# Two layers of dilated attention and GeGLU: chunks of 256 rows throughout, first roots on POOL, low parts on DVE, bulk loads on ACT's queue, a new order

## The chip, the cores and the metric

The kernel runs on one core of a Trainium2 chip. The metric is the device time of one execution in microseconds; the number compared is the median of several runs. A profiled execution has a time of its own and a span, from its first to its last instruction.

## The reference

Four sublayers are applied to x (2048 rows of 512 numbers): attention, feed-forward, and both again with the same weights. Every one has a layer norm in front and a residual around it.

```python
x = x + A(layernorm(x), wqkv, wo)              # wqkv 512 x 1536, wo 512 x 512
x = x + B(layernorm(x), w_gate, w_up, w_down)  # 512 x 1792, 512 x 1792, 1792 x 512
x = x + A(layernorm(x), wqkv, wo)
x = x + B(layernorm(x), w_gate, w_up, w_down)

# A: 32 heads of 16; row s sees the 8 rows s, s-2, ..., s-14 (those below 0 are masked)
qkv = h @ wqkv
logits[s, w] = (q[s] . k[s - 2*w]) / 4
o[s] = sum_w softmax(logits[s])[w] * v[s - 2*w]
A = o @ wo
# B:
B = (gelu(h @ w_gate) * (h @ w_up)) @ w_down
```

## The kernel before

**Chunks.** Because the window steps by 2, even and odd rows never meet. A chunk is `128*J` rows of one parity; `TILES` (line 36) gives the sizes J of both layers: `[1, 1, 2, 2, 2]` in the first, `[2, 2, 2, 2]` in the second, each for both parities. The first layer has 10 chunks, four of them of 128 rows, the second 8 of 256 rows.

**Numbers in two parts.** TensorE multiplies float16. Each operand is a high part (rounded) and a low part (the rest); a product is three passes: high by high, high by low, low by high. Weights are scaled by powers of two first, found from their largest magnitudes: `prep_q`, `prep_f`, `prep_o` and `prep_d` (lines 485 to 598) load a weight (`load`, line 461, on SP's queue), take magnitudes (`absmax` on DVE, L469; `abssum` on ACT, L479), get exponents (`exponents`, L373 to L393, with a transpose on PE, L380), and `split` each block of 128 rows. `split` has three ways: "v", ACT makes the high part from the raw block (L425) and DVE the low part (L430); "p", ACT scales the raw block in place (L436), ACT makes the high part (L446), POOL the low part (L450); the third, POOL scales. Only w_q uses "v". w_q's raw blocks lie in the space of w_d, so w_d is loaded after w_q is split.

**A chunk's way.** `attention_inputs` (line 767): load rows (`load_xa`, three buffers, L654), `norm` (line 662): statistics on DVE (L677, L681), then the reciprocal root by an integer first guess and three Newton steps, 13 small DVE instructions (L704 to L723); ACT normalises (L752); `split_transpose` (line 728) makes high (ACT, L735) and low part (POOL, L739) and turns them with a transposing DMA on SP (L743) into `ax`; PE projects, per half of the heads and row tile in 12 matmuls of 512 columns and 12 of 256 (L763 with w_q), ACT evicts to `stg` (L802), SP stores to DRAM (L813). `attention` (line 820): per group of 8 heads SP loads q and windows of k and v (L840); DVE multiplies (L858), sums (L865), softmax (L876 to L911, ACT's exponential L897), multiplies with v (L917), adds up (L928, L933); the result is split and transposed into `ot`. `feed_forward` (line 945): output projection (L763 with w_o), residual on DVE (L970), `norm` again, `bx`; then seven steps of two column blocks: gate and up (L763 with w_g, w_u), GELU on ACT (L1018), product on DVE (L1026), high part on ACT (L1035), low part on POOL (L1040), down projection (L1051); last the residual (L1064) and a store (L1072) to `xs`, from which the second layer reads, or to the output.

`passes` (L763) issues all matmuls but the down projection, so in the profile these groups are told apart by their tiles.

**The order.** Nothing is issued in the order of this text. Each operation is a node in `Graph` with its engine, a duration, the keys that it reads and writes, buffers to take (`Lease`) and a priority. `plan` (line 138) places node after node on a model of the five engines: of those that can start, the earliest; among those within `WAIT` = 0.3 us of it, one whose priority number is over `SOON` = 20 smaller goes first. It models one DMA stream, and holds a load on SP back until the stream's backlog is under `QUEUE` = 4 us. The instructions are then written out in that order (lines 1096 to 1099), and every engine executes its own in order; an instruction whose data is late holds all behind it. Priorities are in us: the feed-forward pass of a chunk is due at T, which starts at 100 and grows by 38 per 128 rows; attention at T - 90 and on, first inputs of the first chunks 8 apart, later ones at T - 170 (lines 1078 to 1094).

Of the kernel before, what the change touches and what calls it, by code (L numbers as in the profile page):

```python
# [35 lines left out]
TILES = ([1, 1, 2, 2, 2], [2, 2, 2, 2])  # L36
# [46 lines left out]
QUEUE = 4.0  # L83
# [168 lines left out]
def dilated_attention_geglu(ctx: ExitStack, tc: tile.TileContext, x, wqkv, wo, wg, wu, wd, out):  # L252
# [208 lines left out]
    def load(dst, src, kb, w, prio, r=()):  # L461
        return g.add(
            "SP", T_ISSUE + 0.0006 * kb, lambda: nc.sync.dma_start(dst, src), r=r, w=w, kb=kb, prio=prio
        )
# [95 lines left out]
    def prep_o(prio, how):  # L560
        for k in range(KT):
            load(w_o.raw(k), wo[k * P : (k + 1) * P], 256, [(P_o_lease, k)], prio)
        for k in range(KT):
            h = k // (KT // 2)
            abssum(
                am_o[:, h, k % (KT // 2) : k % (KT // 2) + 1], w_o, k, (P_o_lease, k), ("am_o", k), prio + 5
            )
        e = exponents("o", am_o, [("am_o", k) for k in range(KT)], prio + 5)
        su, cst["s_wo"] = meet(
            "o", e, e_v, -127 - 19, [("o", "e"), ("s_log", 0), ("s_log", 1)], prio + 5  # L570
        )
        for k in range(KT):
            h = k // (KT // 2)
            split(w_o, k, su[:, h : h + 1], ("su_o", 0), how[k % len(how)], prio + 6, (P_o_lease, k))

    def load_d(prio):
        for i in range(NF):
# [3 lines left out]
                r=[("q", b) for b in range(2 * KT)],  # L581
# [80 lines left out]
    def norm(xs_of, prio):  # L662
# [12 lines left out]
        for j in range(J):  # L675
# [13 lines left out]
        ts, stt = nc.vector.tensor_scalar, nc.vector.scalar_tensor_tensor
# [2 lines left out]
        def op(fn, r, w):
            def emit():
                st, mv, cs = view()
                fn(mv, cs)
# [6 lines left out]
        g.add(  # L702
            "DVE port", 0.15,
            lambda: ts(view()[2][V], view()[1][:, :, 1], EPS, 2.0 ** (-2 * LX), op0=ALU.add, op1=ALU.mult),  # L704
            r=[(lease, *k) for k in mvs], w=[(lease, V)], prio=prio,
        )
        op(
            lambda mv, c: ts(
                c[Y].bitcast(I32), c[V].bitcast(I32), -0.5, float(0x5F3759DF), op0=ALU.mult, op1=ALU.add
            ),  # L710
            [V], [Y],
        )
        op(lambda mv, c: ts(c[HF], c[V], -0.5, None, op0=ALU.mult), [V], [HF])
        for k in range(3):
            dst = Y if k < 2 else SC
            op(lambda mv, c: nc.vector.tensor_mul(c[WK], c[Y], c[Y]), [Y], [WK])
            op(lambda mv, c: nc.vector.tensor_mul(c[WK], c[WK], c[HF]), [HF], [WK])
# [410 lines left out]
```

## Time and profile before

| | us |
|---|---|
| median of 3 runs | 1308.7 |
| lowest, highest | 1306.49, 1309.39 |
| the profiled execution, its own time | 1306.3 |
| its span | 1304.5 |
| busy in it: PE | 1230.2 (94%) |
| DVE | 1025.8 (79%) |
| ACT | 542.2 (42%) |
| POOL | 388.9 (30%) |
| mean granted TensorE clock | 0.98 |

PE is the row of matmuls and PEld that of weight loads beside them. A busy PE need not be PE at its peak, since matmuls are pipelined and their ends are modelled; how fast they follow one another is seen in the chain and the timeline. Idle time of an engine that is not the bound costs nothing by itself. SPq is SP's queue of DMA issues. Lines such as L763 are lines of the kernel before.

### The profile page before, as it was taken

Reading aid. Unit: us, or ns where it says so; the run is one execution under the profiler, and the core shown is the slowest. Engines: PE = TensorE matmul, PEld = TensorE weight load, DVE = VectorE, ACT = ScalarE, POOL = GpSimd, SP = SyncE. Lnnn points to the kernel's source line nnn. Section 1 sums busy time; section 2 is a strip of 40 time slices with the busy share of each in tenths; the row PEclk is TensorE's granted clock in tenths of the full one; section 3 lists DMA queues with packets and bytes.
Section 4 is the critical chain, followed back from the end, with each engine's and each line's share of the span. In section 5 each row is a group of like instructions: output and inputs, shape, how many; then the busy total and the mean of one; then the engine's idle time right before and its main releaser. Section 6 shows DMA issues by size and latency. Waiting matters only on the chain.

```text
span 1304.5 us, 23267 instructions
## 1 busy us (share of the span) xinstructions
PE 1230.2 (94%) x9322; PEld 861.2 (66%) x9322; DVE 1025.8 (79%) x1762; ACT 542.2 (42%) x832; POOL 388.9 (30%) x307
## 2 busy tenths in 40 slices
PE   2796889998699999999999999999999999999998
PEld 1453558775575777767757777765677677667775
DVE  7878878999998898898998888934889898886211
ACT  5587465443334352435434343332444342322211
POOL 1374263332333242423313322211232224222111
PEclk9897999999799999999999999999999999999999
DMA  9977825774538443335439343317834433231000
GB/s 328 357 212 203 243 82 167 230 181 150 132 112 192 138 122 122 121 122 149 137 129 245 87 121 111 129 41 177 228 81 130 123 122 103 90 120 41 17 17 17
DMA packets 205581, 183.58 MB, mean 141 GB/s; under 512 B 108928, under 2 KB 170368, under 8 KB 205472
## 3 DMA queue, kind: packets, MB, share of 16 engines
q1 hardware_dynamic: 205408, 181.97, 48.0%
q8 instruction: 73, 1.20, 0.4%
q14 instruction: 36, 0.29, 0.1%
q10 hardware_dynamic: 64, 0.11, 0.0%
HBM read 123.21 MB, written 33.67 MB: 120 GB/s over the span
## 4 chain that ended last, share of the span: by engine, by line
PE 74%; DMA 0%; DVE 0%; DVEq 0%; issue 0%; SPq 0%
PE pg L763 54%; PE pd L1051 19%; DMA bx<-hl 0%; DVE x L1064 0%; DVEq L1123 0%; SPq L743 0%
## 5 line engine op out<-in xcount | busy, mean ns | idle before, releaser
L763 PE MATMUL pg<-bx,w_g 128*128 128x256 f16 (+1 forms) x3024 | 338.0, 262 | 20.6 <-DMA bx<-hl 16.1
L763 PE MATMUL pg<-bx,w_u 128*128 128x256 f16 (+1 forms) x3024 | 337.2, 262 | 0.0
L763 PEld LDWEIGHTS <-w_g 128*128 128x128 f16 x3024 | 272.3, 98 | 69.3 <-issue 17.1
L1051 PE MATMUL pd<-w_d,gh 128*128 128x512 f16 x1344 | 310.4, 380 | 5.6 <-POOL w_d L450 5.5
L763 PEld LDWEIGHTS <-w_u 128*128 128x128 f16 x3024 | 271.7, 98 | 26.9
L1040 POOL TENSOR_TENSOR gh<-g,gh 128x512 f16<-128x512 f32 (+1 forms) x126 | 168.3, 1336 | 398.4 <-ACT gh L1035 375.9
L763 PE MATMUL pg<-w_q,ax 128*128 128x512 f16 (+1 forms) x1536 | 262.6, 333 | 23.9 <-DMA ax<-hl 20.4
L763 PEld LDWEIGHTS <-ax 128*128 128x128 f16 x1536 | 152.3, 99 | 134.7 <-DMA ax<-hl 22.5
L1051 PEld LDWEIGHTS <-gh 128*128 128x128 f16 x1344 | 130.9, 98 | 144.6 <-issue 8.0
L1026 DVE SCALAR_TENSOR_TENSOR g<-pg,small,g 128x512 f32<-128x512 f32 (+2 forms) x144 | 89.0, 629 | 151.9 <-ACT g L1018 148.6
L1018 ACT ACTIVATE g<-pg,small 128x512 f32<-128x512 f32 (+2 forms) x144 | 83.5, 593 | 228.7 <-PE pg L763 227.8
L917 DVE TENSOR_TENSOR prod<-v,lg 128x1024 f32<-128x1024 f32 x128 | 165.3, 1315 | 0.9
L739 POOL TENSOR_TENSOR hl<-xn,hl 128x512 f16<-128x512 f32 x64 | 84.1, 1322 | 268.6 <-ACT hl L735 241.9
L858 DVE TENSOR_TENSOR prod<-k,q 128x2048 f32<-128x2048 f32 (+1 forms) x72 | 152.1, 2112 | 3.1 <-DMA k<-qkvd 2.5
L928 DVE TENSOR_TENSOR prod<-prod 128x512 f32<-128x512 f32 (+2 forms) x144 | 151.3, 1051 | 1.6
L865 DVE TENSOR_REDUCE lg<-prod 128x128 f32<-128x2048 f32 (+1 forms) x72 | 146.8, 2039 | 0.7
L739 POOL TENSOR_TENSOR hl<-o,hl 128x256 f16<-128x256 f32 (+1 forms) x72 | 81.5, 1133 | 209.4 <-ACT hl L735 157.8
L1035 ACT CAST gh<-g 128x512 f16<-128x512 f32 (+1 forms) x126 | 71.8, 570 | 77.5 <-DVE g L1026 75.6
L802 ACT ACTIVATE stg<-pg 128x768 f32<-128x768 f32 x64 | 51.6, 811 | 125.8 <-PE pg L763 120.4
L1018 ACT ACT_TABLE_LOAD x53 | 68.0, 1283 | 80.8 <-PE pg L763 80.3
L763 PE MATMUL pg<-w_o,ot 128*128 128x512 f16 x384 | 85.8, 379 | 0.0
L897 ACT ACT_TABLE_LOAD x52 | 66.7, 1283 | 0.9
(71 smaller groups left out, 717.5 us busy)
## 6 DMA issues: line engine op xcount, KB each, us to landing
k<-qkvd SPq DMA_DIRECT2D x56, 576.0 KB, 4.1
v<-qkvd SPq DMA_DIRECT2D x56, 576.0 KB, 3.4
qkvd<-stg SPq DMA_DIRECT2D x64, 384.0 KB, 3.6
k<-qkvd SPq DMA_DIRECT2D x16, 512.0 KB, 4.3
v<-qkvd SPq DMA_DIRECT2D x16, 512.0 KB, 3.9
q<-qkvd SPq DMA_DIRECT2D x56, 128.0 KB, 2.0
xa<-in_A_x_dram SPq DMA_DIRECT2D x16, 256.0 KB, 5.2
xa<-xs SPq DMA_DIRECT2D x16, 256.0 KB, 6.1
```

The lines of the kernel that those rows point to most:

```text
L739: "POOL", t_pool(n), lambda: nc.gpsimd.tensor_sub(lo(), src(), hi()),
L763: nc.tensor.matmul(pt, a, b, start=i == 0, stop=i == n - 1)
L858: nc.vector.tensor_mul(pr, win, q.tile()[:, 0:J].unsqueeze(2).to_broadcast([P, J, W, P]))
L865: lambda lgv=lgv: nc.vector.tensor_reduce(lgv(), pr.rearrange("p j w (h d) -> p j w h d", d=DH), axis=AX.X, op=ALU.add),
L897: lambda lgv=lgv, scale=scale: nc.scalar.activation(lgv(), lgv(), AF.Exp, scale=scale),
L917: lambda j=j, v=v, lg=lg: nc.vector.tensor_mul(prod[:, j].rearrange("p w (h d) -> p w h d", d=DH), v.tile()[:, j : j + W].rearrange("p w ( ...
L928: lambda a=a, b=b: nc.vector.tensor_add(pr[:, :, 0:a], pr[:, :, 0:a], pr[:, :, a:b]),
L1018: lambda sel=sel, h=h, pg=pg, gt=gt: nc.scalar.activation(gt.tile()[:, sel, 0:N], pg.tile()[:, sel, 0:N], AF.Gelu_apprx_tanh, scale=cst["s ...
L1026: lambda sel=sel, h=h, pg=pg, gt=gt: nc.vector.scalar_tensor_tensor(gt.tile()[:, sel, 0:N], pg.tile()[:, sel, JM * P : JM * P + N], cst["c ...
L1035: lambda gt=gt, gh=gh: nc.scalar.copy(gh.tile()[:, 0, :, 0:N], gt.tile()[:, :, 0:N]),
L1040: lambda gt=gt, gh=gh: nc.gpsimd.tensor_sub(gh.tile()[:, 1, :, 0:N], gt.tile()[:, :, 0:N], gh.tile()[:, 0, :, 0:N]),
L1051: nc.tensor.matmul(pd.tile()[:, j], gh.tile()[:, a, i, cs], wd_of(f, b), start=f == 0 and n == 0, stop=f == NF - 1 and n == 2,)
```

## The change

It has five parts.

1. `TILES` gives all chunks of both layers 256 rows: 8 chunks a layer.
2. `norm` gets an engine. For the attention inputs, all but those of the very first chunk, the small instructions after the statistics are eight on POOL, with a power function in place of the guess and the Newton steps. The norm before the feed-forward pass stays on DVE.
3. Gate and up are split by way "v" in place of "p".
4. `load` can issue on ACT's queue: the loads of w_g, w_u, w_o and w_d (34 DMAs) go there. Loads of x and w_q stay on SP. The planner models two streams that share the rate.
5. Priorities come from a table `AT`; weight loads and weight preparation have separate ones, and the first magnitudes are taken first.

```diff
-TILES = ([1, 1, 2, 2, 2], [2, 2, 2, 2])
+TILES = ([2, 2, 2, 2], [2, 2, 2, 2])
...
+AT = dict(
+    lq0=0.0, lq1=1.4, lf0=6.0, lo=42.0, lf1=52.1, ld=60.0, pq0=-787.8, pq1=2.6, pf0=21.6, po=53.4, pf1=59.2,
+    pd=130.5, x0=-1000.0, first=0.0, tile=9.1, ahead=8.5, lead=218.0, norm=300.0, proj=18.6, half=14.0,
+    row=8.0, att=90.0, hg1=6.5, hg2=12.0, kv=33.0, xl=30.6, gu=5.6, start=51.1, step=39.1,
+)
...
-QUEUE = 4.0
+QUEUE = {"SP": 4.0, "ACT": 8.0}
...
-        dma_free, port_free, table = 0.0, 0.0, None
+        dma, port_free, table = {"SP": 0.0, "ACT": 0.0}, 0.0, None
...
-                    if e == "SP" and n.size is not None and not n.urgent:
-                        t = max(t, dma_free - QUEUE)
+                    if n.size is not None and not n.urgent:
+                        t = max(t, dma[e] - QUEUE[e])
...
-                begin = max(t + occ, dma_free)
-                dma_free = begin + n.size / DMA_RATE
-                n.done = dma_free + DMA_FIXED
+                other = "ACT" if e == "SP" else "SP"
+                begin = max(t + occ, dma[e])
+                both = min(max(0.0, dma[other] - begin), 2 * n.size / DMA_RATE)
+                dma[e] = begin + n.size / DMA_RATE + both / 2
+                dma[other] += both / 2
+                n.done = dma[e] + DMA_FIXED
...
+    root = sb.tile([P, JM], F32, name="root")
+    nc.gpsimd.memset(root, -0.5)
...
-    def load(dst, src, kb, w, prio, r=()):
-        return g.add(
-            "SP", T_ISSUE + 0.0006 * kb, lambda: nc.sync.dma_start(dst, src), r=r, w=w, kb=kb, prio=prio
-        )
+    def load(dst, src, kb, w, prio, r=(), on="SP"):
+        eng = nc.sync if on == "SP" else nc.scalar
+        return g.add(on, T_ISSUE, lambda: eng.dma_start(dst, src), r=r, w=w, kb=kb, prio=prio)
...
+        else:
+
+            op(lambda m, v, c: ts(c[V], v, EPS, None, op0=ALU.add), mvs, [V])
+            op(lambda m, v, c: tt(c[Y], c[V], root[:, 0:J], op=ALU.pow), [V], [Y], 0.4 + 0.17 * J)
+            op(lambda m, v, c: tt(c[WK], c[Y], c[Y], op=ALU.mult), [Y], [WK])
+            op(lambda m, v, c: tt(c[WK], c[WK], c[V], op=ALU.mult), [V], [WK])
+            op(
+                lambda m, v, c: ts(
+                    c[WK], c[WK], -(2.0 ** (LX - 1)), 1.5 * 2.0**LX, op0=ALU.mult, op1=ALU.add
+                ),
+                [], [WK],
+            )
+            op(lambda m, v, c: tt(c[SC], c[WK], c[Y], op=ALU.mult), [WK, Y], [SC])
+            op(lambda m, v, c: tt(c[HF], m, c[SC], op=ALU.mult), [SC], [HF])
+            op(lambda m, v, c: ts(c[BI], c[HF], -1.0, None, op0=ALU.mult), [HF], [BI])
...
-        nl, sb_of = norm(xt, prio - 300)
+        nl, sb_of = norm(xt, prio - AT["norm"], "DVE" if l + c == 0 else "POOL")
...
-            prio = T - 90 + (10 if J == 2 else 5) * hg
+            prio = T - AT["att"] + (AT["hg2"] if J == 2 else AT["hg1"]) * hg
...
-    prep_f(0, 25.0, "p")
-    prep_o(40.0, "p")
+    prep_f(0, AT["pf0"], "v")
+    prep_o(AT["po"], "p", AT["lo"])
...
-    prep_f(1, 60.0, "p")
+    prep_f(1, AT["pf1"], "v")
...
-    t, first = 100.0, 0.0
+    t, tiles = AT["start"], 0
     for l in range(2):
         for c, (par, t0, J) in enumerate(CHUNKS[l]):
-            attention_inputs(l, c, -1000.0 if l + c == 0 else first if l == 0 and first < 72 else t - 170)
+            if l + c == 0:
+                when = AT["x0"]
+            elif l == 0 and tiles < AT["ahead"]:
+                when = AT["first"] + AT["tile"] * tiles
+            else:
+                when = t - AT["lead"]
+            attention_inputs(l, c, when)
             ot, mark = attention(l, c, t)
             feed_forward(l, c, t, ot, mark)
-            t += 38.0 * J
-            first += 8.0 * J
+            t += AT["step"] * J
+            tiles += J
```

More of the change, by code (lines that the diff above doesn't have):

```diff
@@ L514, in load_f @@
                 i = h * KT + k
-                load(w.raw(i), src[h, k], 448, [(f"r{key}", i)], prio + 0.1 * k)
+                load(w.raw(i), src[h, k], 448, [(f"r{key}", i)], prio + 0.1 * k, on="ACT")
     def prep_f(h, prio, how):
@@ L558, in meet, with prep_o @@
         return su, s
-    def prep_o(prio, how):
+    def prep_o(prio, how, early):
         for k in range(KT):
-            load(w_o.raw(k), wo[k * P : (k + 1) * P], 256, [(P_o_lease, k)], prio)
+            load(w_o.raw(k), wo[k * P : (k + 1) * P], 256, [(P_o_lease, k)], early, on="ACT")
         for k in range(KT):
@@ L565, in prep_o @@
             abssum(
-                am_o[:, h, k % (KT // 2) : k % (KT // 2) + 1], w_o, k, (P_o_lease, k), ("am_o", k), prio + 5
+                am_o[:, h, k % (KT // 2) : k % (KT // 2) + 1], w_o, k, (P_o_lease, k), ("am_o", k), prio
             )
-        e = exponents("o", am_o, [("am_o", k) for k in range(KT)], prio + 5)
+        e = exponents("o", am_o, [("am_o", k) for k in range(KT)], prio)
         su, cst["s_wo"] = meet(
-            "o", e, e_v, -127 - 19, [("o", "e"), ("s_log", 0), ("s_log", 1)], prio + 5
+            "o", e, e_v, -127 - 19, [("o", "e"), ("s_log", 0), ("s_log", 1)], prio
         )
@@ L573, in prep_o @@
             h = k // (KT // 2)
-            split(w_o, k, su[:, h : h + 1], ("su_o", 0), how[k % len(how)], prio + 6, (P_o_lease, k))
+            split(w_o, k, su[:, h : h + 1], ("su_o", 0), how[k % len(how)], prio + 1, (P_o_lease, k))
     def load_d(prio):
@@ L580, in load_d @@
                 w_d.raw(i), wd[i * P : (i + 1) * P], 256, [("rd", i)], prio + 0.1 * i,
-                r=[("q", b) for b in range(2 * KT)],
+                r=[("q", b) for b in range(2 * KT)], on="ACT",
             )
@@ L660, in load_xa, with norm @@
         return got
-    def norm(xs_of, prio):
+    def norm(xs_of, prio, on="DVE"):
         J = len(xs_of)
@@ L687, in norm, with op @@
             g.add("DVE", 0.17, aggr, r=[(lease, "st", j)], w=[(lease, "mv", j)], prio=prio)
[L689 removed]
         V, HF, WK, Y, SC, BI = range(6)
[L692 removed]
+        eng = nc.vector if on == "DVE" else nc.gpsimd
+        ts, tt = eng.tensor_scalar, eng.tensor_tensor
+        stt = nc.vector.scalar_tensor_tensor
+        def op(fn, r, w, occ=None):
             def emit():
[L694 to L695 removed]
+                _, mv, cs = view()
+                fn(mv[:, :, 0], mv[:, :, 1], cs)
@@ L696, in op @@
             return g.add(
-                "DVE port", 0.15, emit, r=[(lease, k) for k in r], w=[(lease, k) for k in w],
-                prio=prio,
+                "DVE port" if on == "DVE" else "POOL", occ or (0.15 if on == "DVE" else 0.19), emit,
+                r=[(lease, *k) if isinstance(k, tuple) else (lease, k) for k in r],
+                w=[(lease, k) for k in w], prio=prio,
             )
         mvs = [("mv", j) for j in range(J)]
[L702 to L717, printed above, removed]
-            op(
-                lambda mv, c, dst=dst: stt(c[dst], c[WK], 1.5, c[Y], op0=ALU.add, op1=ALU.mult),
-                [WK, Y], [dst],
-            )
@@ L797, in attention_inputs @@
                     r=[(ax, j), *(("q", h * KT + k) for k in range(KT))], w=[(pg, 0)],
-                    get=[pg], prio=prio + 25 + 16 * h + 8 * j,
+                    get=[pg], prio=prio + AT["proj"] + AT["half"] * h + AT["row"] * j,
                 )
@@ L947, in feed_forward @@
         N = J * P
-        xt, xl = load_x(l, c, T - 45, order=[mark])
+        xt, xl = load_x(l, c, T - AT["xl"], order=[mark])
         pw = Lease(P_pg)
```

48 lines of the change are left out of this document (33 added, 15 removed).

## The prediction

> **What bounds the kernel now.** I read the page's slices first, then a table of stages, then PE's waits and the chain that ended last. The slices give the busy tenths of PE in fortieths of the span (32.6 us each):
>
> ```profile
> PE   2796889998699999999999999999999999999998
> ```
>
> All gaps but the last lie in the first eleven slices. The table of stages gives length, busy time (and instructions) of PE, weight loads, DVE, ACT and POOL, then granted clock, DMA share and GB/s:
>
> ```profile
> 0.00:60.00 60.00, 30.09 (x133) 14.82 (x134) 47.71 (x151) 31.19 (x48) 13.32 (x18) 0.91 1.02 338
> 60.00:140.00 80.00, 67.23 (x398) 39.21 (x397) 64.69 (x134) 60.42 (x102) 45.21 (x30) 0.91 0.79 231
> 140.00:200.00 60.00, 49.97 (x522) 36.90 (x521) 47.72 (x116) 37.01 (x66) 29.01 (x28) 0.91 0.46 140
> 200.00:340.00 140.00, 123.89 (x1327) 90.09 (x1325) 127.44 (x246) 63.04 (x110) 44.22 (x42) 0.94 0.62 176
> 340.00:640.00 300.00, 300.00 (x2206) 215.90 (x2205) 265.95 (x416) 123.04 (x177) 96.74 (x68) 1.00 0.48 137
> 640.00:940.00 300.00, 300.00 (x2094) 204.66 (x2092) 235.17 (x361) 113.31 (x162) 69.21 (x56) 1.00 0.49 137
> ...
> 1240.00:1304.50 64.50, 59.06 (x436) 42.37 (x433) 8.20 (x12) 9.31 (x15) 8.09 (x8) 0.99 0.05 17
> ```
>
> From 340 us on PE never stops, at full clock; before, it is idle 68.8 us (340 less 30.09, 67.23, 49.97 and 123.89), and 5.4 us at the end: 74.2 in all. Its waits by cause (total, times, longest):
>
> ```profile
> PE pg L763 <- DMA ax<-hl: 20.4, 4, 11.6
> PE pg L380 <- DVE small L373: 18.8, 3, 12.2
> PE pg L763 <- DMA bx<-hl: 16.1, 1, 16.1
> PE pd L1051 <- POOL w_d L450: 5.5, 4, 1.9
> ```
>
> So PE's own work is the bound, plus what it waits for in the first quarter. What that work is at full speed: in the chain (start, length, matmuls) a run of 256-wide matmuls costs 5.24/48 = 0.1092 us each,
>
> ```profile
> 357.89 5.24 PE pg L763 x48
> ```
>
> and one of 512-wide 5.18/24 = 0.2158:
>
> ```profile
> 394.39 5.18 PE pd L1051 x24
> ```
>
> The counts by form (the busy times beside them are of pipelined matmuls and not used):
>
> ```profile
> L1051 PE MATMUL pd<-w_d,gh 128*128 128x512 f16 x1344 | 310.4, 380 | 5.6 <-POOL w_d L450 5.5
> L763 PE MATMUL pg<-bx,w_g 128*128 128x256 f16 x2352 | 290.0, 273 | 16.1 <-DMA bx<-hl 16.1
> L763 PE MATMUL pg<-bx,w_u 128*128 128x256 f16 x2352 | 289.1, 273 | 0.0
> L763 PE MATMUL pg<-w_q,ax 128*128 128x512 f16 x768 | 184.3, 390 | 23.9 <-DMA ax<-hl 20.4 <-ACT w_q L425 1.6 <-DVE w_q L430 1.2
> L763 PE MATMUL pg<-w_q,ax 128*128 128x256 f16 x768 | 96.0, 276 | 0.0
> L763 PE MATMUL pg<-w_o,ot 128*128 128x512 f16 x384 | 85.8, 379 | 0.0
> L763 PE MATMUL pg<-bx,w_u 128*128 128x128 f16 x672 | 48.1, 223 | 0.0
> ```
>
> With every chunk at 256 rows, gate and up (two equal halves) become 2 x (2352 + 672/2) = 5376 matmuls of 256. The new PE work is (5376 + 768) x 0.1092 = 670.9 us plus (1344 + 768 + 384) x 0.2158 = 538.6, together 1209.5; per chunk 75.6, of which projection 15.6, output projection 5.2, feed-forward 54.8. The present work is the same but for halves of 128 in place of 256, which I price at nothing. Then the span holds 1209.5 of work, 74.2 idle and, as the remainder, 20.8 of slow clock (0.91 to 0.94 in those stages) and of starting up after pauses. Only idle and slow time can be gained.
>
> **Part by part. Chunks of 256 rows** take instructions from DVE:
>
> ```profile
> L858 DVE TENSOR_TENSOR prod<-k,q 128x2048 f32<-128x2048 f32 x56 | 130.8, 2336 | 3.1 <-DMA k<-qkvd 2.5
> ...
> L858 DVE TENSOR_TENSOR prod<-k,q 128x1024 f32<-128x1024 f32 x16 | 21.2, 1327 | 0.0
> ```
>
> Two half-size products cost 2 x 1.327 - 2.336 = 0.32 us more than a whole one. Over some 12 instructions and 8 pairs of head groups that is at most 31 us; I take 22, as reductions and short ones will save less; all of it lies before 340 us. The price: the first chunk's attention is twice as long, and no feed-forward pass can start after 128 rows.
>
> **Roots on POOL.** 15 of the 16 first normalisations lose 13 small DVE instructions, which are not only time but are spread out. One such chain, its first and last instruction:
>
> ```profile
> 113.52 0.16 DVE L704 TENSOR_SCALAR nw<-nw 128x2 f32<-128x2 f32 x1
> ...
> 121.47 0.15 DVE L723 SCALAR_TENSOR_TENSOR nw<-nw 128x2 f32<-128x2 f32 x1
> ```
>
> Here 13 x 0.16 = 2.1 us of work took 8.1, queued between attention instructions. POOL's eight, with a power function, are not in the trace. The nearest, a 128-wide and two 512-wide subtractions:
>
> ```profile
> 125.83 0.43 POOL L739 TENSOR_TENSOR hl<-o,hl 128x128 f16<-128x128 f32 x1 [10.68 <-DMA v<-qkvd]
> 126.49 2.27 POOL L739 TENSOR_TENSOR hl<-xn,hl 128x512 f16<-128x512 f32 x2 [0.24 <-POOL hl L739]
> ```
>
> Bounds for eight: near nothing, and 8 x 1.13 = 9 us. I take 8 x 0.43 = 3.4, since two columns are nearest to the small one: between DVE's 2.1 and its 8.1. After 340 us PE's other work hides it; without that cover the upper bound adds 6 us for each of the first four chunks, 24 us.
>
> **Low parts of gate and up on DVE**, priced by those of w_q:
>
> ```profile
> L430 DVE SCALAR_TENSOR_TENSOR w_q<-w_d,small,w_q 128x768 f16<-128x768 f32 x8 | 9.5, 1238 | 0.4 <-ACT w_q L425 0.4
> ```
>
> 16 x 1.238 x 896/768 = 23 us more DVE work before about 170 us. ACT loses a scaling pass,
>
> ```profile
> L436 ACT ACTIVATE w_u<-w_u,small 128x896 f32<-128x896 f32 x8 | 8.3, 1042 | 0.0
> ```
>
> 16 x 1.04 = 17 us, and gains 34 load issues; at half a us each, more than I expect, ACT comes out level. POOL, 45.21 of 80 us busy at its densest, loses 16 low parts; no price. DVE's balance before 340 us: 23 - 22 - 7 x 2.1 = -14 us.
>
> **The sum for the first stretch.** PE's first wait, 18.8 us for the exponents of w_q, I leave: gate and up loads now compete with x and w_q (share 1.02 already), while one other chunk's root chain leaves DVE there. Four us either way. Then 16 row tiles of projection are ready work, 8 x 15.6 = 125 us, and what decides is when DVE releases the first feed-forward passes.
>
> ```profile
> L469 DVE TENSOR_REDUCE small<-w_g 128x1 f32<-128x896 f32 x8 | 8.6, 1072 | 0.0
> ```
>
> ```profile
> L677 DVE BATCH_NORM_STATS2 nw<-xa 128x6 f32<-128x512 f32 x32 | 21.5, 684 | 23.0 <-DMA xa<-in_A_x_dram 16.6 <-DMA xa<-xs 6.4
> ```
>
> ```profile
> L1026 DVE SCALAR_TENSOR_TENSOR g<-pg,small,g 128x512 f32<-128x512 f32 x84 | 62.9, 748 | 115.4 <-ACT g L1018 115.4
> ```
>
> DVE work ahead of the first pass: magnitudes 20 x 1.07 = 21, w_q's low parts 9.5, the new low parts 23, statistics 16 x (0.68 + 0.16) = 13, and some 70 small ones for exponents and scales at 0.16, 11: together 78. Attention: a whole chunk costs DVE (265.95 + 235.17)/600 x 75.6 = 63 now, 61 with a root gone; less its feed-forward part (11 steps like L1026, 8.2, statistics 1.7, a root 2.1) and first statistics (1.7) leaves 47. So 125 us of work; DVE was idle 140 - 47.71 - 64.69 = 27.6 in the first 140 us, and I allow 25. Attention of chunk 0 ends near 150; of chunk 1, at the 91% busy of 200 to 340 us (127.44/140), 61/0.91 = 67 later, at 217. From the last attention add
>
> ```profile
> 312.15 0.43 DVE L933 TENSOR_TENSOR o<-prod 128x256 f32<-128x256 f32 x1
> ```
>
> over the output projection to the first gate matmul
>
> ```profile
> 316.47 5.34 PE L763 MATMUL pg<-w_o,ot 128*128 128x512 f16 x24
> 337.92 2.29 PE L763 MATMUL pg<-bx,w_g 128*128 128x256 f16 x10 [16.11 <-DMA bx<-hl]
> ```
>
> it took 25.8 us; I take 24. So the second pass starts near 241. PE's ready work ends at 19 + 125 + 54.8 + 2 x 5.2 + 6 of slow clock = 215, and layer 1's first projection can fill some 6 us: 20 us idle. By the third pass (217 + 67 + 24 = 308) PE has 215 + 20 + 54.8 + 5.2 + 15.6 = 311: it is ahead, and stays so, as DVE's 67 a chunk is under PE's 75.6. Earlier waits on ax are inside these 20, since PE must wait for DVE anyhow.
>
> Span: 1209.5 + 18.8 start + 20 + 5.4 end + 10 slow clock (half of 20.8) = 1263.7, against 1304.5. The profiled run took 1306.3, 1.8 more than its span, and the median of three is 1308.7, 2.4 above that: about 1267 us.
>
> **The rivals.** *Nothing left to wait for* (0.17): loads come sooner, DVE idles little, and the second half's weight work fits behind chunk 0's attention; 1267 - 20 - 4 = 1243, to 1251. For: part of DVE's idle time is waits for x. Against: the 24 us path into each pass stays.
>
> *The projection waits stay* (0.12): x rows and transposes land as late as now, because all loads share one DMA capacity. For: share 1.02 and 338 GB/s in the first 60 us, with the same bytes to move. Then the 20.4 us on ax come on top: 1287. The Trainium skill, DMA: Bandwidth & Descriptors, section Issuing engines are not separate DMA queues, says that DMAs started by different engines run on the same 16 DMA engines and interleave, and that a second issuing engine only saves the time of issuing; by that rule this rival is the likelier one, with 1287. No trace here has two load queues at work at once.
>
> *ACT stands in front* (0.09, slower): an issue can itself wait for an older transfer,
>
> ```profile
> SPq L463 <- DMA w_d<-in_A_wqkv_dram: 3.8, 4, 1.7
> ```
>
> here SP's, before loads that need nothing of w_d; and SP has waited for a transfer that ACT had issued:
>
> ```profile
> SPq L654 <- DMA qkvd<-k: 1.8, 1, 1.8
> ```
>
> On ACT such a wait holds what is queued behind it (hi parts of w_q, evictions of stg, casts, exponentials), and with them PE and DVE. 34 loads x 1.7 = 58 us at worst, 1325; it turns gain into loss once some 42 us of it fall on PE's path. Against: this is SP's largest such row, and ACT is busy only 31.19 + 60.42 of the first 140 us.
>
> *The order is no better* (0.05): the pauses move but add up to the same, 1303 to 1311.
>
> **How the numbers follow.** The forecast has 0.57, with 1253 to 1284 as its own range. The range leaves out the slow rival and the far end of the fast one: 1246 to 1296. Under 0.2% (1306.1 to 1311.3) counts as no change, about what a measurement can tell. Faster takes the forecast, the first two rivals and 0.01 of the fourth, 0.87; same 0.04; slower 0.09.
>
> **What would show it.** Right: PE without a stop from about 310 us or earlier; 10 to 25 us of pauses between 100 and 250 us, released by bx; no 128-wide gate matmuls; ACT without long waits on DMA. Wrong: ACT waiting on DMA over 20 us in the first 100; pauses on ax over 15 us; POOL's root chain above 9 us; any pause after 340 us; a first projection after 24 us.

## The result, and the profile after

| | before | after |
|---|---|---|
| median, us (runs) | 1308.53 (4) | 1275.7 (4) |
| lowest, highest | 1306.49, 1309.39 | 1274.46, 1276.76 |
| profiled execution, its own time | 1306.3 | 1276.52 |
| its span | 1304.5 | 1274.7 |
| PE idle up to 340 us | 68.8 | 48.5 |
| first projection matmul | 19.71 | 33.39 |
| first matmul of a feed-forward pass | 156.03 (128 rows) | 172.3 (256 rows) |
| PE, DVE, ACT, POOL busy | 1230.2, 1025.8, 542.2, 388.9 | 1220.2, 986.5, 498.7, 437.0 |

The ratio of after to before is 0.9751, 95% interval 0.9734 to 0.9768. The changed kernel is 33 us faster. The forecast was 1267, so 9 us of the expected 42 did not come.

Lines are from here on those of the changed kernel: L396 is the transpose for the exponents, L441 and L446 high part and low part by way "v", L479 a load, L484 and L494 magnitudes on DVE and ACT, L746 to L758 POOL's roots, L785 ACT's normalisation, L796 `passes`, L835 the eviction to `stg`, L891 the product of q and k, L1084 the down projection.

The slices of the changed kernel's page, PE busy in tenths of a fortieth of the span (31.9 us):

```profile
PE   0779999999999999999999999999999999999998
```

The pauses have drawn together at the front: the first slice is empty, the next two are at 7, and from the fourth on PE is full. The table of stages, with the columns as before (busy time of PE, weight loads, DVE, ACT, POOL; granted clock, DMA share, GB/s):

```profile
0.00:60.00 60.00, 20.86 (x88) 9.96 (x89) 40.69 (x90) 26.46 (x42) 13.66 (x31) 0.97 0.92 295
60.00:140.00 80.00, 73.18 (x438) 43.26 (x436) 63.71 (x100) 45.38 (x83) 38.88 (x43) 0.96 1.02 268
140.00:200.00 60.00, 58.23 (x426) 41.41 (x424) 53.38 (x85) 39.37 (x61) 27.52 (x28) 1.00 0.61 162
200.00:340.00 140.00, 139.21 (x995) 96.99 (x994) 123.90 (x168) 59.72 (x87) 65.62 (x50) 1.00 0.51 140
...
1240.00:1274.70 34.70, 28.68 (x204) 19.59 (x201) 4.54 (x7) 5.33 (x9) 4.61 (x4) 0.99 0.04 16
```

The first 60 us are worse than before (PE 20.86 busy against 30.09), the other three stages better (73.18, 58.23, 139.21 against 67.23, 49.97, 123.89), and the clock is back to 1.00 by 140 us. Between 340 and 1240 us PE doesn't stop. PE's waits (total, times, longest):

```profile
PE pg L396 <- DVE small L389: 21.6, 1, 21.6
PE pg L796 <- ACT w_q L441: 12.1, 4, 11.3
PE pg L796 <- ACT stg L835: 6.8, 1, 6.8
PE pg L796 <- DMA ax<-hl: 6.2, 2, 4.5
...
PE pg L796 <- DMA bx<-hl: 0.8, 1, 0.8
```

Before, 20.4 and 16.1 us were waits for ax and bx. Now 33.7 of 48.5 us are waits for w_q's exponents and high part, that is, the start. The rest is mostly ACT's eviction (6.8) and ax (6.2).

So the span is PE's 1209.5 us of work (the prediction's figure) + 32.9 idle before the first projection (33.39 less the 0.45 of one transpose) + 15.6 of other pauses up to 340 us (48.5 - 32.9) + 6.0 at the end (34.70 - 28.68) + 10.7 left over = 1274.7. Beside the same work the prediction had 18.8 + 20 + 5.4 + 10, the last called slow clock.

**What held the start.** ACT's timeline (start, length, engine, line, what; ACTq are its DMA issues):

```profile
1.62 0.45 ACTq L479 DMA_DIRECT2D w_g<-in_B_w_gate_dram  x1
5.95 0.34 ACTq L479 DMA_DIRECT2D w_u<-in_B_w_up_dram  x1
...
15.63 1.28 ACT L785 ACT_TABLE_LOAD   x1 [15.63 <-DMA w_d<-in_A_wqkv_dram]
...
25.76 0.82 ACT L494 ACTIVATE pd<-w_d 128x768 f32<-128x768 f32 x1 [4.47 <-issue]
...
32.02 0.33 ACTq L479 DMA_DIRECT2D w_g<-in_B_w_gate_dram  x1
32.40 0.94 ACT L441 ACTIVATE w_q<-w_d,small 128x768 f16<-128x768 f32 x1 [5.70 <-DMA w_d<-in_A_wqkv_dram]
```

An issue itself takes 0.3 to 0.5 us. But in the first 15 us there are gaps of up to 3.9 us (2.07 to 5.95) between them in which ACT does nothing. Its normalisation (L785) needs only rows of x and a root. The root is ready at 11.3 us, as DVE's last instruction for it shows, so that ACT's idle time before that did not delay the normalisation:

```profile
11.16 0.16 DVE L741 SCALAR_TENSOR_TENSOR nw<-nw 128x2 f32<-128x2 f32 x1
```

From then on five more issues (12.20 to 15.27) and a table load stand in front of the normalisation, which runs at 16.93. Why an issue stands can be read in the trace: every DMA of SP and of ACT signals one of eight semaphores (100 to 104 and 106 to 108), which the two engines share, and an issue waits until the earlier DMA on its semaphore is complete. The issue of w_g at 32.02 waits for semaphore 101, which the last block of w_q, issued by SP at 23.59, signals. The chain of work shows where this decides the start; the last of w_q's loads, an issue on ACT's queue, and then the high part that PE waits for:

```profile
23.59 8.41 DMA w_d<-in_A_wqkv_dram
32.02 0.33 ACTq L479
32.40 0.95 ACT w_q L441
```

The first high part of w_q needs the exponents, which DVE had by 24.8 us:

```profile
24.62 0.15 DVE L428 TENSOR_SCALAR small<-small 128x1 int32<-128x1 f32 x1
```

Instead it ran at 32.40, behind an issue of w_g that stood until a transfer was done that neither the issue nor this high part needs: the last block of w_q, issued by SP at 23.59 and complete at 32.0. So the high part ran 7.6 us after its exponents, and for 5.7 of these ACT stood idle at that one issue. Here a load on ACT was cheap to issue and dear to stand behind.

### The profile page after: what moved, and what is told of

It reads as the page before. It is cut to its first block, busy times and chain, and to the rows that moved or that the text cites. A ratio compares the mean times of both kernels' runs of the same rounds, so it can differ in the third digit from the quotient of the medians.

```text
span 1274.7 us, 21387 instructions
## 1 busy us (share of the span) xinstructions
PE 1220.2 (96%) x8650; PEld 847.9 (67%) x8650; DVE 986.5 (77%) x1435; ACT 498.7 (39%) x754; POOL 437.0 (34%) x388
## 4 chain that ended last, share of the span: by engine, by line
PE 91%; DMA 4%; DVE 3%; POOL 1%; SPq 1%; issue 0%; ACT 0%; POOLq 0%; ACTq 0%; DVEq 0%
PE pg L796 68%; PE pd L1084 23%; DMA w_d<-in_A_wqkv_dram 2%; DMA ax<-hl 1%; DMA k<-qkvd 1%; DVE w_q L446 1%; DVE small L484 1%; DMA bx<-hl 0%; DVE nw L692 0%; POOL w_o L466 0%; SPq L776 0%; DVE w_u L446 0%; DVE prod L891 0%; DVE x L1097 0%; DVE w_g L446 0%
## 5 line engine op out<-in xcount | busy, mean ns | idle before, releaser
L796 PE MATMUL pg<-bx,w_g 128*128 128x256 f16 x2688 | 330.0, 273 | 0.8 <-DMA bx<-hl 0.8
L796 PE MATMUL pg<-bx,w_u 128*128 128x256 f16 x2688 | 330.0, 273 | 0.0
L1073 POOL TENSOR_TENSOR gh<-g,gh 128x512 f16<-128x512 f32 x112 | 172.1, 1537 | 422.8 <-ACT gh L1068 400.6
L1084 PE MATMUL pd<-w_d,gh 128*128 128x512 f16 x1344 | 306.4, 379 | 0.6 <-POOL gh L1073 0.6
L796 PEld LDWEIGHTS <-w_g 128*128 128x128 f16 x2688 | 262.9, 98 | 48.5 <-DMA bx<-hl 1.1
L796 PE MATMUL pg<-w_q,ax 128*128 128x512 f16 (+1 forms) x1536 | 261.8, 331 | 25.5 <-ACT w_q L441 12.1
L796 PEld LDWEIGHTS <-w_u 128*128 128x128 f16 x2688 | 263.0, 98 | 30.4
L796 PEld LDWEIGHTS <-ax 128*128 128x128 f16 x1536 | 151.9, 99 | 135.8 <-issue 26.3
L1084 PEld LDWEIGHTS <-gh 128*128 128x128 f16 x1344 | 131.4, 98 | 141.3 <-POOL gh L1073 1.0
L1059 DVE SCALAR_TENSOR_TENSOR g<-pg,small,g 128x512 f32<-128x512 f32 (+1 forms) x128 | 85.9, 680 | 171.7 <-ACT g L1051 167.6
L1051 ACT ACTIVATE g<-pg,small 128x512 f32<-128x512 f32 (+1 forms) x128 | 79.7, 636 | 255.6 <-PE pg L796 243.9
L891 DVE TENSOR_TENSOR prod<-k,q 128x2048 f32<-128x2048 f32 x64 | 150.2, 2347 | 4.4 <-POOL w_o L466 3.4
L961 DVE TENSOR_TENSOR prod<-prod 128x1024 f32<-128x1024 f32 (+1 forms) x128 | 145.6, 1138 | 1.9
L898 DVE TENSOR_REDUCE lg<-prod 128x128 f32<-128x2048 f32 x64 | 145.7, 2277 | 0.9
L772 POOL TENSOR_TENSOR hl<-o,hl 128x256 f16<-128x256 f32 x64 | 87.1, 1362 | 138.4 <-ACT hl L768 135.5
L835 ACT ACTIVATE stg<-pg 128x768 f32<-128x768 f32 x64 | 51.4, 810 | 135.1 <-PE pg L796 120.8
L1068 ACT CAST gh<-g 128x512 f16<-128x512 f32 x112 | 69.0, 616 | 76.9 <-DVE g L1059 73.7
L796 PE MATMUL pg<-w_o,ot 128*128 128x512 f16 x384 | 85.5, 379 | 0.0
L1051 ACT ACT_TABLE_LOAD x45 | 57.7, 1283 | 67.2 <-PE pg L796 67.0
L796 PEld LDWEIGHTS <-ot 128*128 128x128 f16 x384 | 37.6, 98 | 42.3
```

Of the source, the lines that this page charges most:

```text
L772: "POOL", t_pool(n), lambda: nc.gpsimd.tensor_sub(lo(), src(), hi()),
L796: nc.tensor.matmul(pt, a, b, start=i == 0, stop=i == n - 1)
L835: lambda pg=pg, stg=stg: nc.scalar.activation(stg.tile().rearrange("p t g c -> p (t g c)"), pg.tile().rearrange("p b c -> p (b c)")[:, 0:768],
L891: nc.vector.tensor_mul(pr, win, q.tile()[:, 0:J].unsqueeze(2).to_broadcast([P, J, W, P]))
L898: lambda lgv=lgv: nc.vector.tensor_reduce(lgv(), pr.rearrange("p j w (h d) -> p j w h d", d=DH), axis=AX.X, op=ALU.add),
L961: lambda a=a, b=b: nc.vector.tensor_add(pr[:, :, 0:a], pr[:, :, 0:a], pr[:, :, a:b]),
```

## The experiments

The theory after the result: the time is set by PE's idle time up to 340 us, and the changed kernel loses at the start because ACT is held by its issues. The rivals: the start is late because gate and up share DMA with w_q, whoever issues them; and the start doesn't matter, since DVE's work ahead of the first pass decides anyhow.

All twelve, with PE's idle time up to 340 us, the first projection and the first gate matmul of each profiled execution:

| kernel | median, us | ratio to before, 95% | idle to 340 | first projection | first gate |
|---|---|---|---|---|---|
| after | 1275.70 | 0.9734-0.9768 | 48.5 | 33.4 | 172.3 |
| e1: after, all loads on SP, order laid out anew by the planner | 1267.47 | 0.9668-0.9709 | 37.0 | 21.8 | 165.4 |
| e2: after, gate, up and w_o loads only after w_q's first high part | 1282.21 | 0.9799-0.9830 | 52.2 | 19.8 | 179.4 |
| e3: after, old tiles | 1305.87 | 0.9970-0.9994 | 67.2 | 26.7 | 155.3 |
| e4: before, new tiles | 1301.58 | 0.9942-0.9975 | 70.5 | 20.9 | 176.0 |
| e5: after, all roots on DVE | 1282.75 | 0.9779-0.9824 | 52.3 | 32.2 | 172.4 |
| e6: after, low parts on POOL | 1295.14 | 0.9882-0.9911 | 65.8 | 33.4 | 186.5 |
| e7: tiles and priorities only | 1291.68 | 0.9857-0.9887 | 57.9 | 22.4 | 186.7 |
| e8: e1, w_q's second half prepared first | 1270.37 | 0.9696-0.9725 | 42.5 | 21.4 | 164.2 |
| e9: e8, up's magnitudes on ACT | 1283.54 | 0.9797-0.9827 | 51.0 | 21.0 | 171.6 |
| e10: e1 with the old priorities | 1297.80 | 0.9907-0.9937 | 69.1 | 22.7 | 185.8 |
| e11: after's own order, SP issues all | 1265.84 | 0.9670-0.9703 | 38.9 | 24.5 | 161.2 |
| e12: e2's own order, SP issues all | 1277.00 | 0.9741-0.9797 | 46.9 | 19.3 | 174.9 |

In every kernel with whole chunks, the profiled span less the idle time in this table is 1224 to 1233 us (after 1274.7 - 48.5 = 1226.2; e11 1263.1 - 38.9 = 1224.2; e7 1291.1 - 57.9 = 1233.2): the first part of the theory holds to within 9 us over a range of 36 us of results. An edit of one line can alter many instructions' places, since the planner lays out the whole order anew; only e11 and e12 keep the order of another kernel.

### e1: all loads on SP

```diff
-                load(w.raw(i), src[h, k], 448, [(f"r{key}", i)], prio + 0.1 * k, on="ACT")
+                load(w.raw(i), src[h, k], 448, [(f"r{key}", i)], prio + 0.1 * k)
```

The same in the two other places.

> The changed kernel with all weight loads back on SP's queue, nothing else edited (the planner lays the order out for it). Theory A, the late start (first projection at 33.4 us against 19.7 before) is made by the bulk loads on ACT, which take DMA share from x and w_q and hold ACT while they wait for older transfers: the first projection comes at 18 to 22 us and the time falls to about 1262. Rival B, ACT's queue is what took away the waits on ax (20.4 us before, 6.2 after): the start is early but 10 to 15 us of pauses on ax come back between 40 and 140 us, 1272 to 1280. Rival C, the start is late because magnitudes and statistics were put in another order: the first projection stays at 30 or later, 1275.

It was faster than the changed kernel, 1267.47 against 1275.7 us (intervals apart). PE's waits:

```profile
PE pg L396 <- DVE small L389: 16.8, 1, 16.8
PE pg L796 <- DMA ax<-hl: 12.5, 4, 4.3
```

The start is back at 21.8 us and no long wait on ACT is left; the waits for ax are 6.3 us longer than after's 6.2, those for ACT's eviction 4.8 shorter. The loads on ACT's queue were a loss. This doesn't separate the holding of ACT from the sharing of DMA, since both the order of the bytes and the issuer changed.

### e2 and e12: gate and up after w_q

```diff
-                load(w.raw(i), src[h, k], 448, [(f"r{key}", i)], prio + 0.1 * k, on="ACT")
+                load(w.raw(i), src[h, k], 448, [(f"r{key}", i)], prio + 0.1 * k, r=[(("q", 0), "hi")], on="ACT")
```

The same for w_o.

> The changed kernel, but the loads of w_g, w_u and w_o on ACT's queue may be placed only after the first high part of w_q. Theory A: first projection at 18 to 20 us; what the loads then hold on ACT (the second chunk's normalisation stands behind ten of them) gives back some of the 14 us, so 1262 to 1270. Rival C: the start stays at 30 or later and the time at 1275. If early loading of gate and up is itself needed (their magnitudes fill DVE's idle time), the start is gained but pauses before the first feed-forward pass grow by as much: 1275.

The first projection came at 19.8 us, 13.6 earlier than after's, and the run was slower, 1282.21. The early start, bought with late gate and up weights, was worth nothing here. Two causes were left: ACT still held, only later, or the weights themselves late. e12 keeps e2's instructions in their order and lets SP issue the loads.

> The order of e2 (loads of gate, up and w_o only after the first high part of w_q), but SP issues the 34 loads. If what cost that run its early start was that ACT's stream stood behind issues: first projection near 20 us again, the pauses on bx and ax shrink (no single one of bx over 5 us), and the time is 1263 to 1270. If the loss was that gate and up arrive late, whoever issues them: the pauses on bx (13 us) and ax (9 us at most) stay, and the time is 1276 to 1283.

It took 1277.0 us: 5 us less than e2, its interval just below that one's, so the holding of ACT has a part. But the pauses stayed:

```profile
PE pg L796 <- DMA ax<-hl: 13.4, 4, 6.3
PE pg L796 <- DMA bx<-hl: 12.9, 1, 12.9
```

So the larger part of the loss lies in the order that e2 and e12 share, in which gate and up come late. DVE does their magnitudes, low parts and the attention in one stream. The first magnitude of gate runs at 23.9 us here and at 6.9 in the changed kernel, the last of up at 70.5 and 71.8, and the first product of q and k starts at 75.3 and 76.5: 14 us of earlier start have left next to no trace in it. That the late weights are the cause is read from these dates; the order differs from the changed kernel's in more than them. The chain of the pause on bx, from the end of PE's work at 235.04 us to the first matmul of the second pass:

```profile
235.07 1.41 DVE x L1097 x2
...
240.48 0.81 ACT xn L785
...
243.10 1.44 POOL hl L772 x2
244.54 3.23 DMA bx<-hl
...
247.91 12.15 PE pg L796 x92
```

It is the serial way into a feed-forward pass, from the last sum of the residual over statistics, root, normalisation, low part and transposing DMA, 12.9 us with no other work beside it: attention was so late that PE had nothing else.

### e11: the same order, another issuer

```diff
-        eng = nc.sync if on == "SP" else nc.scalar
+        eng = nc.sync
```

> The changed kernel in its own order, planned as if the 34 loads were on ACT, but SP issues them at the same places of the program. So the same bytes compete with x and w_q in the same order, and ACT is never held by an issue. If holding ACT makes the late start: first projection at 20 to 26 us in place of 33.4, and 1262 to 1270. If the shared DMA capacity makes it: still 29 us or later, 1273 to 1277. SP, now with all DMAs, may be late with transposes: pauses on ax over 10 us would show it.

The planner's order is the changed kernel's; only the engine that issues the 34 loads differs. 1265.84 us, the lowest median of all, though not distinguishable from e1's 1267.47 (intervals overlap). PE's waits:

```profile
PE pg L396 <- DVE small L389: 20.2, 1, 20.2
PE pg L796 <- DMA ax<-hl: 9.5, 3, 5.8
PE pg L796 <- ACT w_q L441: 4.5, 4, 3.8
PE pg L396 <- ACT stg L835: 3.3, 1, 3.3
```

and ACT's timeline at the same two places as above:

```profile
11.87 0.81 ACT L785 ACTIVATE xn<-xa,nw 128x512 f32<-128x512 f32 x1 [4.03 <-DVE nw L741]
...
23.50 0.93 ACT L441 ACTIVATE w_q<-w_d,small 128x768 f16<-128x768 f32 x1 [0.43 <-DVE small L428]
```

The first normalisation and the first high part now wait for DVE, which they need, and the high part runs at 23.50 in place of 32.40. The first projection is 8.9 us earlier (24.5 against 33.4), the first gate matmul 11.1, and the span 11.6. SP does nothing but issue DMAs in this kernel, so an issue that waits there holds only other transfers. The issuer also changes when each load starts: w_q's blocks landed after a median of 7.0 us here and of 9.8 in the changed kernel. So e11 gives what the issuer costs in all, and no run separates ACT's standing from the later landing; the 5.7 us in front of the high part are ACT's standing by the changed kernel's own trace. The 2.7 us from 24.5 to e1's 21.8 go with the order of the loads, not with the issuer.

ACT's queue costs once more, later. Of these waits of ACT in the changed kernel

```profile
ACT L785 <- DMA w_d<-in_A_wqkv_dram: 15.6, 1, 15.6
ACT stg L835 <- DMA k<-qkvd: 10.7, 1, 10.7
...
ACT w_q L441 <- DMA w_d<-in_A_wqkv_dram: 5.7, 1, 5.7
```

the second holds an eviction that needs nothing of k: it stands behind eight issues of w_d, from 76.42 to 87.6 us. PE's pause of 6.8 us, up to 88.5 us, hangs on it; its chain:

```profile
79.17 8.11 DMA k<-qkvd
87.30 0.33 ACTq L479
...
87.68 0.82 ACT stg L835
88.54 3.57 PE pg L796 x8
```

### e3, e4, e7, e10: tiles and order

e3 puts the old `TILES` into the changed kernel, e4 the new ones into the kernel before.

```diff
-TILES = ([2, 2, 2, 2], [2, 2, 2, 2])
+TILES = ([1, 1, 2, 2, 2], [2, 2, 2, 2])
```

> The changed kernel with the old chunk sizes in the first layer (four chunks of 128 rows), nothing else edited. Theory D, in the first 340 us DVE's progress decides and 256 rows save DVE about 22 us: the time rises by 10 to 20 us, to 1286 to 1296, with pauses between 140 and 340 us. Rival E, the gain came from order and queue, and small chunks only let the first pass start sooner: 1265 to 1278.

> The kernel before with all chunks of 256 rows, nothing else edited. Theory D: the 22 us that DVE saves shorten the pauses of 16.1 and others before 340 us; 1285 to 1298. Rival E: the larger first chunk makes the first pass later by as much as DVE saves, and the old order keeps its pauses on ax: 1303 to 1315.

Alone the new tiles gain some 6 us (0.9942 to 0.9975), although the idle time to 340 us is no smaller (70.5 against 68.8); what shrank is the span less that idle time, from 1235.7 to 1230.7. PE's waits of e4 (its lines are those of the kernel before):

```profile
PE pg L763 <- DMA bx<-hl: 25.5, 3, 21.1
PE pg L763 <- DMA ax<-hl: 23.8, 5, 8.8
```

Before, the longest on bx was 16.1; here PE waits 21.1 us for the first pass, at 155 to 176 us, as no pass of 128 rows comes ahead of it. In e3, where the order was laid out for the old tiles by the new priorities, all but some 2 us of the change's gain is gone. So the tiles are worth 6 or 30 us by what stands beside them.

e7 is e1 without roots and low parts: only tiles and priorities.

```diff
-        nl, sb_of = norm(xt, prio - AT["norm"], "DVE" if l + c == 0 else "POOL")
+        nl, sb_of = norm(xt, prio - AT["norm"], "DVE")
...
-    prep_f(0, AT["pf0"], "v")
+    prep_f(0, AT["pf0"], "p")
```

and the same for the second half.

> Of the change only the chunk sizes and the order (loads on SP's queue, roots on DVE, low parts on POOL). Chunk sizes alone made 1301.6, and with roots on POOL, low parts on DVE and the order, but loads on SP, 1267.5. If the order is what the sizes lacked: 1265 to 1278. If moving work off DVE and POOL is needed for it: 1285 to 1300, with pauses on bx between 150 and 260 us as in the run with sizes alone (25.5 us).

1291.68 us, 10 below e4: what the new priorities, with the planner's new model, give by themselves. The waits for ax, 27.4 us, are as large as ever. Step by step, then: tiles 1301.6, priorities 1291.7, roots and low parts 1267.5 (e1), ACT's queue back up to 1275.7. In e10 the old priorities stand in the new table, in e1:

```diff
-    lq0=0.0, lq1=1.4, lf0=6.0, lo=42.0, lf1=52.1, ld=60.0, pq0=-787.8, pq1=2.6, pf0=21.6, po=53.4, pf1=59.2,
...
+    lq0=0.0, lq1=4.0, lf0=10.0, lo=40.0, lf1=45.0, ld=60.0, pq0=0.0, pq1=4.0, pf0=25.0, po=45.0, pf1=60.0,
...
```

> The version with all loads on SP (1267.5), but with the priorities of the kernel before put into the table: due times, lead, first magnitudes and loads as they were. Chunk sizes, roots on POOL and low parts on DVE stay. If the laying out anew is worth as much as the step from 1301.6 (sizes alone) to 1291.7 (sizes and order): 1275 to 1280. If most of the gain is the work moved off DVE, POOL and ACT and the order hardly matters: 1265 to 1272.

1297.8 us, 30 more than e1. One pause makes it, in PE's timeline:

```profile
175.91 4.40 PE L796 MATMUL pg<-w_q,ax 128*128 128x512 f16 x10 [37.71 <-DMA ax<-hl]
```

The old priorities ask for the later chunks' inputs late, and PE, ahead of its first pass, finds no projection ready for 37.7 us. So the order is worth 10 us where roots and low parts are as before, and 30 where they are new.

### e5 and e6: roots and low parts undone

```diff
-        nl, sb_of = norm(xt, prio - AT["norm"], "DVE" if l + c == 0 else "POOL")
+        nl, sb_of = norm(xt, prio - AT["norm"], "DVE")
```

> The changed kernel with all first normalisations' roots on DVE as before, the rest as changed. Theory F, DVE's progress decides the early part: 7 chains of 2.1 us more on DVE before 340 us, and spread out again; the time rises by 5 to 15 us, 1281 to 1291, with pauses before the first two feed-forward passes. Rival G, with the late start DVE is ahead of PE (the second pass waited 0.8 us), so the roots are hidden: within 4 us of 1275.7.

1282.75 us, 7 more. The start is nearly the same (32.2). Two waits appear that the changed kernel doesn't have:

```profile
PE pg L796 <- DMA ot<-hl: 8.4, 3, 6.1
PE pg L796 <- DVE nw L734: 6.1, 1, 6.1
```

The second is put down to a Newton step, one of the 13 small instructions (L734) that stand between others on DVE. In return the 6.8 us for ACT's eviction are gone and the waits on ax are 1.0 in place of 6.2, so that PE's idle time up to 340 us is only 3.8 us larger (52.3 against 48.5), of 8.1 us between the two spans. The run shows what the roots are worth, not that these two waits are all of it.

```diff
-    prep_f(0, AT["pf0"], "v")
+    prep_f(0, AT["pf0"], "p")
```

and the same for the second half.

> The changed kernel with gate and up split by ACT, ACT and POOL as before. DVE loses 19.2 us of low parts (9.1 + 10.1 in the changed profile), POOL gains some 32 and ACT 14. Theory F: less DVE work early, 3 to 10 us faster, 1266 to 1273. Rival H, ACT and POOL are then late with normalised rows and with the weights themselves: more waits on ax, or a wait of the first pass on w_g or w_u; 1278 to 1290.

1295.14 us, 19 more. In the stage from 60 to 140 us of this run

```profile
60.00:140.00 80.00, 64.58 (x388) 38.08 (x387) 60.66 (x78) 61.37 (x101) 60.94 (x59) 0.91 0.78 227
```

ACT (61.37) and POOL (60.94) are as busy as DVE (60.66), where the changed kernel has 45.38, 38.88 and 63.71. On POOL a low part takes 2.1 us there, on DVE in the changed kernel 1.1 to 1.3:

```profile
L466 POOL TENSOR_TENSOR w_u<-w_u 128x896 f16<-128x896 f32 x8 | 16.8, 2101 | 2.1 <-ACT w_u L462 2.1
```

```profile
L446 DVE SCALAR_TENSOR_TENSOR w_u<-w_u,small 128x896 f16<-128x896 f32 x8 | 10.1, 1257 | 0.8 <-ACT w_u L441 0.8
...
L446 DVE SCALAR_TENSOR_TENSOR w_g<-w_g,small 128x896 f16<-128x896 f32 x8 | 9.1, 1142 | 0.9 <-ACT w_g L441 0.9
```

The low parts share POOL and ACT with the chunk inputs' own parts, and the inputs come late: PE's longest waits for ax and bx in that run are 13.9 and 9.3 us. The move puts 19 us more on DVE, the engine by which the prediction dated the first passes, and it gains 19.

### e8 and e9: can the first pass come earlier still

e8 gives the second half of w_q's preparation almost the first half's priority, in e1; e9 moves up's eight magnitudes from DVE to ACT, in e8.

```diff
-    ... pq0=-787.8, pq1=2.6, pf0=21.6, ...
+    ... pq0=-787.8, pq1=-780.0, pf0=21.6, ...
```

> The version with all loads on SP, and the preparation of the second half of w_q put ahead of the magnitudes of gate and up (one priority). In that version PE waits 4.3 us for low parts of w_q and 2.7 us on ax at the start. Theory, what PE waits for at the start is paid in full because PE is without a stop from 150 us on: 4 to 8 us less than 1267.5, so 1260 to 1264. Rival, the later magnitudes delay gate and up, and the first pass waits as much longer: 1266 to 1272.

1270.37 us, not distinguishable from e1 or slightly slower (intervals overlap). PE was busier up to 140 us (30.90 + 79.01 = 109.9 against 105.3 in e1), and then stood:

```profile
164.16 2.08 PE L796 MATMUL pg<-bx,w_g 128*128 128x256 f16 x9 [12.39 <-DVE lg L944]
```

The first pass came at 164.2, 1.2 us earlier than in e1, because DVE hadn't come further. Idle time moved from one place to another.

```diff
-                absmax(am_f[:, h, n, k : k + 1], w, i, (f"r{key}", i), ("am_f", h, n, k), prio)
+                (abssum if n else absmax)(am_f[:, h, n, k : k + 1], w, i, (f"r{key}", i), ("am_f", h, n, k), prio)
```

> The version with loads on SP and w_q's second half first (1270.4, where PE stood 12.4 us before the first feed-forward pass), with the eight magnitudes of up taken by ACT as sums instead of DVE as maxima (the power of two that scales up is then another one). Theory J, once the start is early DVE's progress up to the first pass decides: 8.6 us of DVE work gone, the first gate matmul at 156 to 160 in place of 164.2, the time 1261 to 1267. Rival, PE's projections and the waits on ax set the start of the first pass: 1268 to 1273.

1283.54 us, 13 more than e8. If DVE's amount of work alone set the first pass, eight magnitudes at 1.07 us less on DVE should have brought it forward by up to 8.6 us; it came 7.4 later (171.6). The waits:

```profile
PE pg L796 <- DMA ax<-hl: 19.8, 3, 11.1
...
PE pg L796 <- DMA ot<-hl: 11.6, 2, 7.8
```

The output projection began at 124.7 us and stopped for ot twice, so what came late seems to be not the weights but the inputs and the attention's own transposes, whose data pass through ACT. The theory of DVE's work alone fell here. Whether the order that the planner made of it or ACT's eight added sums by themselves did the harm, this run can't tell.

## Why the prediction came out as it did

The forecast was 1267 with a range of 1246 to 1296; 1275.7 lies in it, on the side of faster, and the likeliest case was right in the large: pauses are removed from the first quarter, while PE's work bounds the rest. But the pauses that stayed are not the ones that it named, and some of its terms came out by luck.

- **PE's work, 1209.5 us, and 10 us of slow clock.** Together they fit: with the idle times measured, 10.7 us is left. But the granted clock of the stages accounts for at most 60 x 0.03 + 80 x 0.04 + 34.7 x 0.01 = 5.3 us of it; where the rest lies was not traced. This remainder, 20.8 before, is 10.1 of the 29.8 us by which the span fell, beside a clock that rose from 0.91 to 0.97, 0.96 and 1.00 in the first three stages. The prediction halved it without a reason, so its size is partly luck.
- **Start, 18.8 us, "four us either way".** The step that failed: 32.9. It is the term of the sum that was mis-sized by 14.1 us; the other terms together came out 3.1 lower (middle 15.6 for 20, end 6.0 for 5.4, remainder 10.7 for 10), so the span is 11.0 over the 1263.7 of the sum. Of the 14.1, e11 gives 8.9 to the issuer alone, by the same order; 2.7 more go with e1's order of the loads, and the last 2.5 are gone in e12 (19.3), where gate and up are loaded after w_q. (The sum gives 1267.9 with its 1.8 and 2.4 added, which the prediction rounds to 1267.)
- **"ACT comes out level".** As to busy time it did better (498.7 against 542.2 in all). An issue's own 0.3 to 0.5 us was within the half a microsecond allowed. But it was priced by the time of issue, where the price is the wait in front of it.
- **The rival that ACT stands in front.** It had 0.09 and 42 us of loss before the sign turns. Its mechanism took place: 15.6 + 5.7 + 10.7 us of ACT's waits are put down to transfers that the work behind them doesn't need, and 4.5 more to issues. Of the 15.6, 11.3 lie before the first root was ready, so that the normalisation lost only the rest. On the time it costs about 10 us (1275.7 less e11's 1265.84), not 42, because PE's path doesn't meet all of it. The prediction treated as a rival what was a term of the likeliest case.
- **The rival that the projection waits stay.** ax waits fell from 20.4 to 6.2 us, though the DMA share was 0.92 and 1.02. The Trainium skill, DMA: Bandwidth & Descriptors, section Issuing engines are not separate DMA queues, was quoted there for it. Its rule itself agrees with the runs: a second issuing engine brought nothing that e11 hasn't, with one issuer. What was wrong was to conclude that the waits on ax then stay; with all loads from SP they are 12.5 us in e1, 27.4 without roots and low parts (e7) and 47.7 with the old priorities (e10), so it is the work in front of them and its order that decide them here, far more than the number of queues (6.2 with two and 9.5 with one, by the same order, in e11).
- **20 us of idle ahead of the second pass.** Not there: PE waited 0.8 us for bx, where the second pass started at 248.87. The prediction had PE out of work from 215 on; the start moved that 14 us later, and some 15 us of other pauses in PE's first 90 us, above all for ACT's eviction (6.8) and ax (6.2), moved it as much again, so that PE and DVE met. The 15.6 us that stand where the sum had 20 are therefore other pauses at another place, and their likeness in size is luck. The pause does appear where the start is early and attention isn't: 12.9 us in e12, 12.4 (for the first pass) in e8. So the start and this pause are not two terms to be added, and this is why 14 us of start cost less than 14.
- **DVE's dates.** The first output projection was put at about 154 and came at 145.7, the second at 221 and came at 227.2, the second pass at 241 and came at 248.9. DVE needed 81.5 us from one to the next, against 67: in between lie low parts of the second half (the last starts at 184.4), which the prediction counted before the first attention. They are at most 8 x 1.2 = 10 us of the 14; the rest was not traced.
- **Chunks of 256 rows, 22 us less on DVE.** The run that changes only the tiles (e4) has DVE busy for 1017.4 us against 1025.8 before: 8.5, well under half. No date of the sum is worked out from the 22.
- **Low parts on DVE, 23 us.** Measured 9.1 + 10.1 = 19.2, one sixth less.
- **POOL's root chain, 3.4 us between 0 and 9.** The chain that isn't disturbed, its first, power and last instruction:

```profile
42.05 0.23 POOL L746 TENSOR_SCALAR nw<-nw 128x2 f32<-128x2 f32 x1 [20.74 <-DVE nw L696]
42.37 0.72 POOL L747 TENSOR_TENSOR nw<-nw,root 128x2 f32<-128x2 f32 x1
...
44.55 0.24 POOL L758 TENSOR_SCALAR nw<-nw 128x2 f32<-128x2 f32 x1
```

It takes 2.7 us; over all 15 chains the means of the eight instructions (0.61, 0.83, 0.61, 0.53, 0.53, 0.20, 0.37, 0.47) add up to 4.1. From first to last instruction, with other work between, the eight chains that start before 300 us took 2.7 to 19.6 us, two of them over 9. ACT waited for a chain's last instruction 14.5 us in the whole run.

Of the signs named in advance, PE without a stop from 310 us on came true (from 249), and so did the missing gate matmuls of 128 columns. Pauses of 10 to 25 us on bx and an ACT without long DMA waits did not. Two of the signs of error came: a first projection after 24 us, and ACT waiting more than 20 us on DMA within the first 100 (32.0 by its rows, 20.7 without the 11.3 before the root). Both point at the one step above. A root chain above 9 us came only from first to last instruction, as just said, not as work.

## What to carry to other kernels

A load that is moved to a compute engine's queue is priced by what can stand in front of its issue, not by the issue: list what is behind it in that engine's stream, and give the bulk loads to an engine without arithmetic unless the gaps are known. Here keeping the changed kernel's own order and issuing from SP (e11) gains 10 us on the change as made, 1265.84 against 1275.7.

When two engines in turn set the date of an early stage, idle time gained at one place turns up at the next (e2, e8, e12); add such pauses as "the later of", not as a sum, and judge parts of a change together, as the same tiles were worth 6 us alone and 30 beside the rest.

## What was unexpected of the hardware

An issue on ACT stood some 5 us for the completion of another engine's transfer, SP's 8.41 us load of w_q, and arithmetic stood behind it. The Trainium skill, DMA: Bandwidth & Descriptors, section Anatomy of one DMA — SWDGE (gpsimd) path, says that a DMA's wait on a semaphore is served by the issuing sequencer before dispatch, not by the DMA engines. The trace agrees: the issue runs at 32.02, when the transfer that it waits for is complete (23.59 + 8.41 = 32.00).

The w_q loads took a median of 9.8 us to land in the changed kernel, 7.0 in e11 and 5.0 in e1 by their tables of DMA issues, for the same blocks of 384 KB. From two queues these blocks landed 2.8 us later than from one by the same order of instructions; that the queues themselves are the reason is not shown, as the moments of issue differ too.

POOL's two-column instructions take 0.19 to 0.24 us undisturbed and 0.7 to 0.8 with a power function, beside DVE's 0.16; moving the small work of 15 roots there, off a crowded DVE, was worth 7 us (e5).
